# A fused RWKV, cosine-MoE and soft-MoE kernel: weight landing buffers, score matmuls in quarters, decayed state on another engine, and a new order list

## The chip, the cores and the metric

The kernel runs on one core of one Trainium2 chip. The metric is the device time of one execution in microseconds. Three runs of the kernel before took 516.99, 517.70 and 518.56 us; the median is 517.7 us. The engines are named as in the profile: PE (matrix multiply) with its weight loads PEld, DVE (vector), ACT (scalar, with the function tables), POOL, and SP, whose queue issues every DMA of this kernel.

## The reference

Three stages follow each other. All inputs are float32 but the two MoE weights `w_in` and `w_out`, which come as float64.

```python
def _attn_ref(r, k, v, w, u):            # B=4, H=8, S=768, D=48
    for t in range(S):
        cur = einsum('bhd,bhe->bhde', u[None] * kt, vt)
        y[:, :, t] = einsum('bhd,bhde->bhe', rt, state + cur)
        state = wt[..., None] * state + einsum('bhd,bhe->bhde', kt, vt)

def _moe_ref(x, w_in, w_out):            # x: 3072 tokens x 384, d_ff = 2048
    h = x @ w_in
    return (h * cos(h)) @ w_out

def _moe2_ref(x, phi, w1, w2):           # 8 experts, 4 slots each
    logits = x @ phi
    d = softmax(logits, axis=0);  slot_input = d.T @ x
    slot_out[e] = relu(slot_input[e] @ w1[e]) @ w2[e]
    return softmax(logits, axis=1) @ slot_out
```

## The kernel before, in words

The first load is `cs`, the constants (identity, masks). **Attention** runs over 24 blocks of 128 tokens (`j` = 0 to 23, six to a batch), each as two chunks of 64. For a block the steps are: loads of w, k, r, v (`lw lk lr lv lz`), PE transposes of them (`wT kT rT`, four 128x128 transposes each, one PSUM bank each), products of decays by two DVE scans (`scan`, `sp`), scaled keys and receptances (`ks`, `L`), scores `A` (16 matmuls of 64x64 by 64 columns), the masking of the scores into the tile `lt` (`mask`, two `copy_predicated` of 64 partitions by 512, line 214), the transposed keys (`kN`, `ksn`), the chunks' outer products `U` (16 matmuls, two banks, line 239), the decayed state `z` (line 248, one DVE product of 128x192 for each chunk, but a memset for the first chunk of a batch), its copy into `rzs` by ACT (`rz`), the state's update by DVE (`st`, line 256, which reads a bank of `U` and `z`), and the block's output `y` (32 matmuls of 32 columns each), which ACT and DVE split into a high and a low part (`xh`, `xl`).

**The MoE** takes each block's tokens as soon as they are there: for each of 24 token tiles `t` and four banks `q` of 512 features, `h.t.q` (nine matmuls of 512 columns, lines 421 to 423), then ACT, DVE, ACT, DVE (`turns rest cos mul`) make h cos(h), PE transposes it (`gT`), ACT copies it (`gc`) and PE multiplies it by a projection to the 32 slots (`l`). Softmax steps over tokens (`sum lc max exp xt xr xd dT dc ltok E es`) follow for each 256 tokens. After the list, an end part works out the experts and the outputs.

**The weights** come as float64 bit pairs and are decoded on the chip: ACT takes the high word's magnitude (`abs`), DVE shifts it, puts the sign in and joins the low word's bits (`d1 d2a d2b`, lines 329, 334, 342); `w_in` is then split into a rounded part (`whi`, ACT) and a rest (`wn` on PE, `wc` on ACT) that fill the tiles `wu0` to `wu3`, one for each bank `q`. `w_in` lands in eight pieces of 256 columns (the first of them in two halves) in a ring of two raw buffers, one half in the place of `wu0`; of `w_out`, four pieces land two by two in the places of `wu2` and `wu3` and four in the ring. `w_out` pieces are decoded into `wo_sb`, transposed (`oT`, `oc`) and projected (`om pc pT ps`).

**Order.** The text `HEAD` is a list of 1896 steps, written out; it is run through from front to back under a manual schedule, so each engine's queue, and SP's with its DMAs, holds its instructions in the order of the list. A queue works strictly in its order; an instruction waits in front of its queue until its inputs are there and its buffer is free. PSUM's eight banks are parted into pools; most attention steps (`wT kT rT kN A U y`, and `wn oT pT`) share the pool `ps_a` of three banks:

```python
ps_h = ...tile_pool(name="ps_h", bufs=2, space=PSUM)    # h
ps_t, ps_l, ps_m: one bank each                          # gT, l, softmax
ps_a = ...tile_pool(name="ps_a", bufs=3, space=PSUM)     # attention, weights
```

Of the kernel before, what the change touches and what calls it, by code (L numbers as in the profile page):

```python
# [21 lines left out]
def rwkv_moe_kernel(ctx: ExitStack, tc: tile.TileContext, r, k, v, w, u, w_in, w_out, phi, w1, w2, cst, out):  # L22
    nc = tc.nc
# [266 lines left out]
    raw_t, a_t, pt_ps, wt_t = {}, {}, {}, {}  # L290

    def part(t, hf):

        if hf is None:
            return t
        t = t.rearrange("p (k f) t -> p k f t", k=KD) if len(t.shape) == 3 else t.rearrange("p (k f) -> p k f", k=KD)
        return t[:, :, hf * 128:(hf + 1) * 128]

    def e_raw(x, n, hf=None):

        if x == "i":
            if hf:
                raw_t[x, n, hf] = wu_p.tile([128, 4 * DM, 2], I32, tag="wu0", name=f"rawi{n}b")[:, 0:768, :]
            else:
                raw_t[x, n, hf] = raw_p.tile([128, 768, 2], I32, tag="raw", name=f"rawi{n}")
            src = w_in[:, n * 256:(n + 1) * 256].bitcast(I32).rearrange("(k p) f -> p k f", p=128)
            dst = raw_t[x, n, hf].rearrange("p (k f) t -> p k (f t)", k=KD)
            if hf is not None:
                src, dst = (v[:, :, hf * 256:(hf + 1) * 256] for v in (src, dst))
            nc.sync.dma_start(dst, src)  # L310
        elif n < 4:
            t = wu_p.tile([128, 4 * DM, 2], I32, tag=f"wu{3 - n // 2}", name=f"rawo{n}")
            src = w_out[n * 256:(n + 2) * 256, :].bitcast(I32).rearrange("(q p) n -> p q n", p=128)
            nc.sync.dma_start(t.rearrange("p (q n) t -> p q (n t)", q=4), src)
            raw_t[x, n, None], raw_t[x, n + 1, None] = t[:, 0:768, :], t[:, 768:1536, :]
        else:
# [555 lines left out]
wc.0.0 st.1.0 wn.0.1 d2b.o.1 z.1.1 abs.o.0 abs.o.2 rz.1.0 y.0 d1.o.0 st.1.1 wc.0.1 d2a.o.0 sr.2 oT.2 ru.2 oc.2 oT.3 xh.0 oc.3 d2b.o.0 rz.1.1 kT.2
d1.o.2 xl.0 oT.1 ks.2 lv.3 oT.0 sp.2 y.1 abs.i.1 oc.1 d2a.o.2 d1.i.1 oc.0 kN.2 d2b.o.2 wT.3 om.0 wf.3 xh.1 d2a.i.1 xl.1 oT.4 ksn.2 oT.5 oc.4 U.2
d2b.i.1 oc.5 z.2.0 raw.i.3 st.2.0 lw.5 whi.1 abs.i.4 z.2.1 bo.2 rT.2 bs.2 st.2.1 L.2 wn.1.0 wc.1.0 lz.3 d1.i.4 wn.1.1 wc.1.1 d2a.i.4 rz.2.0 oT.7
scan.3 A.2 abs.i.3 d2b.i.4 d1.i.3 lk.3 D.2 mask.2 d2a.i.3 raw.i.6 h.0.0 oc.7 whi.4 wn.4.1 d2b.i.3 rz.2.1 wc.4.1 kT.3 turns.0.0 wn.4.0 lw.4 whi.3 lr.3
pc.0 ru.3 abs.i.6 sr.3 raw.i.5 ks.3 wc.4.0 oT.6 sp.3 oc.6 d1.i.6 wn.3.0 rest.0.0 wc.3.0 wn.3.1 lk.4 d2a.i.6 rT.3 wT.4 d2b.i.6 wc.3.1 L.3 z.3.0 wf.4
whi.6 cos.0.0 h.1.0 abs.i.5 scan.4 pT.0 raw.i.7 turns.1.0 wn.6.1 d1.i.5 wc.6.1 wn.6.0 bo.3 wT.5 mul.0.0 wc.6.0 sr.4 d2a.i.5 h.0.1 abs.i.7 d2b.i.5 sp.4
whi.5 bs.3 lz.2 A.3 ps.0 turns.0.1 lr.4 rz.3.0 y.2 wf.5 D.3 xh.2 om.1 rest.1.0 d1.i.7 kN.3 cos.1.0 mask.3 ksn.3 wn.5.0 rest.0.1 cos.0.1 wc.5.0 wn.5.1
mul.1.0 raw.o.4 gT.0.0 wc.5.1 d2a.i.7 kT.4 xl.2 lz.4 d2b.i.7 mul.0.1 abs.o.4 whi.7 U.3 pc.1 ks.4 ru.4 raw.o.5 st.3.0 h.0.2 wn.7.0 d1.o.4 turns.0.2
z.3.1 gc.0.0 d2a.o.4 wn.7.1 rest.0.2 wc.7.1 st.3.1 h.1.1 rT.4 gT.0.1 cos.0.2 abs.o.5 wc.7.0 scan.5 turns.1.1 d2b.o.4 bo.4 lw.6 oT.8 oc.8 mul.0.2  # L880
rest.1.1 sr.5 kN.4 d1.o.5 h.0.3 bs.4 cos.1.1 L.4 mul.1.1 pT.1 rz.3.1 d2a.o.5 lk.5 ksn.4 gc.0.1 y.3 turns.0.3 h.1.2 rest.0.3 oT.9 xh.3 ps.1 cos.0.3
raw.o.7 lv.4 d2b.o.5 oT.11 gT.0.2 z.4.0 turns.1.2 oc.11 lr.5 oc.9 D.4 xl.3 oT.10 oc.10 A.4 rest.1.2 U.4 mul.0.3 l.0.0 sp.5 l.0.1 st.4.0 mask.4 abs.o.7
lw.7 lr.6 z.4.1 om.2 cos.1.2 pc.2 gc.0.2 raw.o.6 mul.1.2 abs.o.6 h.2.0 ru.5 gT.0.3 rz.4.1 rT.5 gc.0.3 pT.2 d1.o.6 h.1.3 ps.2 rz.4.0 d1.o.7 st.4.1 wT.6
d2a.o.6 d2b.o.6 turns.1.3 wf.6 L.5 kT.5 gT.1.1 lz.5 ks.5 d2a.o.7 gc.1.1 lr.7 lw.8 lv.5 oT.12 oT.13 turns.2.0 kN.5 oc.12 d2b.o.7 close rest.1.3 lk.6
bo.5 ksn.5 z.5.0 gT.1.0 l.0.2 gc.1.0 oc.13 A.5 oT.14 gT.1.2 oT.15 bs.5 scan.6 oc.14 D.5 l.1.0 l.1.1 oc.15 cos.1.3 gc.1.2 mul.1.3 ru.6 y.4 rest.2.0
om.3 h.2.1 pc.3 xh.4 pT.3 cos.2.0 mask.5 gT.1.3 bo.6 xl.4 turns.2.1 wT.7 ps.3 U.5 l.1.2 sr.6 mul.2.0 gc.1.3 lv.6 l.0.3 sp.6 rz.5.0 st.5.0 wf.7 l.1.3
z.5.1 sum.0 rz.5.1 rest.2.1 h.2.2 scan.7 rT.6 gT.2.0 cos.2.1 mul.2.1 turns.2.2 L.6 rest.2.2 gc.2.0 kT.6 h.2.3 lk.7 lc.0 bs.6 ks.6 cos.2.2 turns.2.3
sr.7 gT.2.1 lz.6 mul.2.2 kN.6 z.6.0 ksn.6 st.5.1 D.6 rest.2.3 ru.7 gc.2.1 max.0 sp.7 exp.0 A.6 xt.0 U.6 gT.2.2 lr.8 h.3.0 xr.0 xd.0 cos.2.3 st.6.0
bo.7 dT.0 ltok.0 dc.0 mul.2.3 lk.8 gc.2.2 y.5 z.6.1 turns.3.0 l.2.0 rest.3.0 mask.6 l.2.1 xh.5 cos.3.0 E.0.0 h.3.2 rT.7 st.6.1 rz.6.0 xl.5 turns.3.2
rz.6.1 mul.3.0 wT.8 kT.7 L.7 ks.7 gT.2.3 h.3.1 ru.8 rest.3.2 gc.2.3 gT.3.0 A.7 lv.8 E.0.1 l.2.2 bs.7 turns.3.1 z.7.0 bo.8 wf.8 cos.3.2 rest.3.1 y.6  # L890
D.7 lw.10 scan.8 lv.7 lr.9 l.2.3 gc.3.0 mul.3.2 lw.9 l.3.0 cos.3.1 sr.8 kN.7 es.0 sp.8 xh.6 ksn.7 mask.7 mul.3.1 bs.8 h.3.3 rT.8 L.8 kT.8 gT.3.2 h.4.1
# [112 lines left out]
```

## Time and profile before

| | |
|---|---|
| median of three runs | 517.7 us |
| profiled execution | 517.14 us, span 515.4 us, granted clock 0.991 |
| PE busy | 481.4 us, 93% of the span |
| DVE busy | 426.2 us, 83% |
| ACT busy | 318.7 us, 62% |
| POOL busy | 100.2 us, 19% |
| DMA | 67.47 MB, 131 GB/s on average |

Busy time is the time in which at least one instruction of the engine is under way, so a matmul that streams behind another is not counted twice. PE's busy share is low in the first slices of the span and in the last ones; between, it is at 90% or more in every slice. An execution's own time is a little more than its span (517.14 against 515.4 us).

### The profile page before, as it was taken

The page shows a single profiled execution, that of the slowest core. Times are in us where ns is not written, and L with a number is a line of the kernel's source. Part 1 is how long each engine was busy: PE and PEld are TensorE (multiplying, and loading weights), DVE is VectorE, ACT ScalarE, POOL GpSimd, SP SyncE. Part 2 cuts the span into 40 slices and gives each one's busy share as a digit, 9 for nine tenths or more (in the row PEclk, how much of TensorE's full clock was granted, in tenths as well). Part 3 has the DMA queues.
Part 4 walks back from the last instruction along what each step waited for, and adds up shares of the span by engine and source line. Part 5 has one row for each costly group of instructions (what it writes and reads, how often), then busy time and mean ns, then how long its engine had stood idle before and what let it go on. Part 6 is the DMA issues. An engine that isn't in the chain of part 4 may idle for free.

```text
span 515.4 us, 15516 instructions
## 1 busy us (share of the span) xinstructions
PE 481.4 (93%) x6515; PEld 378.3 (73%) x6515; DVE 426.2 (83%) x809; ACT 318.7 (62%) x703; POOL 100.2 (19%) x127
## 2 busy tenths in 40 slices
...
GB/s 208 313 191 139 198 166 203 139 66 45 100 67 68 59 36 93 18 51 76 48 108 4 62 73 23 108 48 95 25 56 17 350 369 39 102 294 336 400 174 269
DMA packets 146325, 67.47 MB, mean 131 GB/s; under 512 B 127184, under 2 KB 134352, under 8 KB 146256
## 3 DMA queue, kind: packets, MB, share of 16 engines
...
q8 instruction: 51, 0.84, 0.7%
q14 instruction: 18, 0.15, 0.1%
...
## 4 chain that ended last, share of the span: by engine, by line
PE 53%; DVE 7%; ACT 3%; issue 1%
PE h L421 9%; PE h L423 8%; PE h L422 8%; PE gT L455 6%; PE l L470 3%; PE E L566 3%; PE A L193 2%; PE hps L754 2%; PE so L794 2%; PE y L267 2%; PE U L239 1%; DVE g L440 1%; PE o L827 1%; PE rT L134 1%; PE kT L134 1%; DVE lt L214 1%
## 5 line engine op out<-in xcount | busy, mean ns | idle before, releaser
L421 PE MATMUL h<-wu,x 128*128 128x512 f32 x288 | 121.4, 422 | 1.4 <-DVE g L448 1.3
L423 PE MATMUL h<-wu,x 128*128 128x512 f32 x288 | 113.2, 393 | 0.0
L422 PE MATMUL h<-wu,x 128*128 128x512 f32 x288 | 112.6, 391 | 0.0
L444 ACT ACTIVATE g<-g,half_pi 128x512 f32<-128x512 f32 (+1 forms) x97 | 69.2, 719 | 32.2 <-DVE g L440 31.6
L436 ACT ACTIVATE g<-h 128x512 int32<-128x512 f32 (+1 forms) x96 | 56.6, 595 | 51.8 <-PE h L423 41.9
L440 DVE SCALAR_TENSOR_TENSOR g<-g,h 128x512 f32<-128x512 int32 (+1 forms) x96 | 64.5, 675 | 18.0 <-ACT g L436 17.6
L448 DVE TENSOR_TENSOR g<-g,h 128x512 f32<-128x512 f32 (+1 forms) x96 | 64.7, 675 | 13.3 <-ACT g L444 12.3
L207 POOL TENSOR_SCALAR_AFFINE_SELECT lt<-bo 64x512 f32<-64x512 f32 x48 | 37.3, 778 | 159.4 <-ACT bo L230 89.6
L421 PEld LDWEIGHTS h<-wu,x 128*128 128x128 f32 x288 | 54.2, 188 | 16.5 <-issue 3.5
L461 ACT COPY gt<-gT 128x512 f32<-128x512 f32 x89 | 51.8, 585 | 19.1 <-PE gT L455 15.7
L423 PEld LDWEIGHTS h<-wu,x 128*128 128x128 f32 x288 | 54.0, 188 | 12.3
L422 PEld LDWEIGHTS h<-wu,x 128*128 128x128 f32 x288 | 54.4, 189 | 8.7
L455 PE MATMUL gT<-cs,g 128*128 128x128 f32 x384 | 57.5, 275 | 0.2
L162 POOL TENSOR_TENSOR ru<-rn,u_b 128x384 f32<-128x384 f32 x24 | 26.2, 1092 | 133.8 <-DMA rn<-in_r_dram 82.9
L455 PEld LDWEIGHTS gT<-cs,g 128*128 128x128 f32 x384 | 44.7, 141 | 8.2 <-issue 1.9
L214 DVE COPY_PREDICATED lt<-cs,A 64x512 f32<-64x512 uint32 x48 | 35.4, 737 | 1.6 <-POOL lt L207 0.3
L253 ACT COPY rzs<-z 64x192 f32<-64x192 f32 x96 | 33.4, 348 | 4.1 <-DVE z L248 3.0
L149 DVE TENSOR_TENSOR_SCAN qt<-wf,one_b 128x520 f32<-128x520 f32 x24 | 30.4, 1267 | 5.8 <-ACT wf L144 5.7
L178 DVE TENSOR_TENSOR lt<-rT,pt 64x512 f32<-64x512 f32 x48 | 32.8, 683 | 0.8 <-PE rT L134 0.2
L470 PE MATMUL l<-gt,p_sb 128*32 128x128 f32 x768 | 30.7, 276 | 0.3 <-DVE gt L461 0.3
L193 PE MATMUL A<-lt,ks 64*64 64x64 f32 x768 | 28.0, 224 | 3.0 <-DVE st_state L256 1.6
L157 DVE TENSOR_TENSOR_SCAN pt<-wf,ini_f 128x520 f32<-128x520 f32 x24 | 30.1, 1256 | 0.1
...
## 6 DMA issues: line engine op xcount, KB each, us to landing
...
rawi<-in_moe_w_in_dram SPq DMA_DIRECT2D x7, 768.0 KB, 5.0
wn<-in_w_dram SPq DMA_DIRECT2D x24, 192.0 KB, 4.4
kn<-in_k_dram SPq DMA_DIRECT2D x24, 192.0 KB, 4.0
rn<-in_r_dram SPq DMA_DIRECT2D x24, 192.0 KB, 3.9
vn<-in_v_dram SPq DMA_DIRECT2D x24, 192.0 KB, 3.8
...
```

Of the source, the lines that this page charges most:

```text
L193: nc.tensor.matmul(ps[64 - 64 * a:128 - 64 * a, s, :], lhsT=ks[k, s, :], rhs=L[k, a, s, :], start=True, stop=True)
L214: nc.vector.copy_predicated(out=lt[j % 2][h, a], mask=mask[h].bitcast(U32).unsqueeze(1).to_broadcast([64, NS, C]), data=ps[h])
L421: nc.tensor.matmul(half[:, f], lhsT=xh[:, c, :], rhs=wh, start=(c == 0), stop=False)
L422: nc.tensor.matmul(half[:, f], lhsT=xl[:, c, :], rhs=wh, start=False, stop=False)
L423: nc.tensor.matmul(half[:, f], lhsT=xh[:, c, :], rhs=wl, start=False, stop=(c == KD - 1))
L436: nc.scalar.activation(gt.bitcast(I32), hp, AF.Copy, bias=0.25, scale=1.0 / TWO_PI)
L440: nc.vector.scalar_tensor_tensor(out=gt, in0=gt.bitcast(I32), scalar=-TWO_PI, in1=hp, op0=ALU.mult, op1=ALU.add)
L444: nc.scalar.activation(gt, gt, AF.Sin, bias=half_pi[:, 0:1])
L448: nc.vector.tensor_tensor(out=gt, in0=gt, in1=hp, op=ALU.mult)
L455: nc.tensor.transpose(ps[:, m * 128:(m + 1) * 128], gt[:, m * 128:(m + 1) * 128], ident)
L461: (nc.vector.tensor_copy if n >= ATT and n % 8 in (1, 2, 5) else nc.scalar.copy)(gt_t[t, q], pend.pop(("gT", t, q)))
L470: nc.tensor.matmul(lps_t[g][32 * m:32 * m + 32, o:o + TB], lhsT=p_sb[:, 4 * q + m, :], rhs=gt[:, m * 128:(m + 1) * 128], start=first, stop ...
```

## The change

Four things change.

1. `w_in` lands by bank in a tile of its own, which takes the place (the tag) of the later `wu` tile of that bank: bank 0 in two DMAs of 256 columns, banks 1 to 3 in one DMA of 512 columns each. `w_out` lands in eight pieces, all through the ring of two. The decode works on whole pieces, with a ring of four decoded tiles (`dec` has 4 buffers, was 2).
2. From block 6 on (`JA = 6`) the scores `A` go to two banks and, for every second segment, to the other 64 output partitions, so that all four pairs of a row half and a column half of the array occur in turn. `mask` is then four `copy_predicated` of 64x256 in place of two of 64x512.
3. From block 8 on (`JZ = 8`) `z` is four ACT instructions of 128x48 with a scale for each partition, in place of one DVE product of 128x192.
4. `HEAD` is a new order of 1890 steps.

```diff
+    JZ = 8
+    JA = 6
-    dec = d_stack.enter_context(tc.tile_pool(name="dec", bufs=2))
+    dec = d_stack.enter_context(tc.tile_pool(name="dec", bufs=4))
     def e_A(j):
-        ps = tps(f"A{j}").rearrange("p (s j) -> p s j", j=C)
+        ps = [tps(f"A{j}_{a}" if j >= JA else f"A{j}").rearrange("p (s j) -> p s j", j=C) for a in range(1 if j < JA else 2)]
         for s in range(NS):
             for a in range(2):
                 k = slice(64 * a, 64 * a + 64)
-                nc.tensor.matmul(ps[64 - 64 * a:128 - 64 * a, s, :], lhsT=ks[k, s, :], rhs=L[k, a, s, :], start=True, stop=True)
+                o = 64 * a if j >= JA and s % 2 else 64 - 64 * a
+                out = ps[0][o:o + 64, s] if j < JA else ps[a][o:o + 64, s // 2]
+                nc.tensor.matmul(out, lhsT=ks[k, s, :], rhs=L[k, a, s, :], start=True, stop=True)
     def e_mask(j):
         for a in range(2):
             h = slice(64 - 64 * a, 128 - 64 * a)
+            if j < JA:
+                ...
+            for c in range(2):
+                o = slice(64 * a, 64 * a + 64) if c else h
+                nc.vector.copy_predicated(out=lt[j % 2][h, a, c::2], mask=..., data=ps[a][o, 0:HP])
     def e_z(j, c):
-            nc.vector.tensor_tensor(out=z, in0=st_state, in1=pc[:, :, c, :].to_broadcast([128, HP, D]), op=ALU.mult)
+            if j < JZ:
+                nc.vector.tensor_tensor(out=z, in0=st_state, in1=pc[:, :, c, :].to_broadcast([128, HP, D]), op=ALU.mult)
+            else:
+                for p in range(HP):
+                    nc.scalar.activation(z[:, p], st_state[:, p], AF.Copy, scale=pc[:, p, c])
+    def e_raw(x, n):
+        if x == "i":
+            q, f = n // 2, slice((n % 2) * 256, (n % 2) * 256 + 256) if n < 2 else slice(0, 512)
+            if q not in rawi_t:
+                rawi_t[q] = wu_p.tile([128, KD * 512, 2], I32, tag=f"wu{q}", name=f"rawi{q}")...
+            ...
+            nc.sync.dma_start(t.rearrange("p k f t -> p k (f t)")[:, :, 2 * f.start:2 * f.stop], src)
+        else:
+            t = raw_p.tile([128, 768, 2], I32, tag="raw", name=f"rawo{n}")
+            ...
 HEAD = """
-lw.0 lk.0 raw.i.2 z.0.0 wT.0 lw.1 kT.0 wf.0 scan.0 raw.i.0.0 abs.i.2 ks.0 sr.0 sp.0 d1.i.2 d2a.i.2 wT.1 lr.0 misc kN.0 ru.0 wf.1 scan.1 ksn.0 d2b.i.2
+raw.i.0 abs.i.0 d1.i.0 raw.i.1 lk.0 lw.0 abs.i.1 raw.i.2 d2a.i.0 d2b.i.0 d1.i.1 d2a.i.1 wT.0 lr.0 wf.0 d2b.i.1 kT.0 lw.1 whi.1 z.0.0 scan.0 lv.0
 ...
-bs.11 rest.7.3 st.11.0 cos.7.3 h.8.0 mul.7.3 kT.12 sp.12 turns.8.0 bs.12 rest.8.0 lw.13 ks.12 h.7.2 z.11.1 gc.7.1 cos.8.0 mul.8.0 lv.13 gT.7.0 D.11
+U.11 gT.6.3 rest.7.3 cos.7.3 h.7.0 st.11.0 mul.7.3 cmb.0.1 h.8.0 kT.12 z.11.1 turns.7.0 cmb.0.4 sp.12 gc.6.3 lv.12 rest.7.0 gT.7.1 cos.7.0 xl.9
 ...
```

## Rows read from the trace of the kernel before

**Rows 1.** Windows: length, busy us (x instructions) by engine, granted clock, DMA share, GB/s.

```profile
0.00:13.00 13.00, 5.04 (x20) 3.72 (x20) 6.40 (x9) 4.91 (x8) 3.65 (x22) 1.00 0.98 207
13.00:77.00 64.00, 50.00 (x651) 35.24 (x652) 61.57 (x92) 40.11 (x82) 19.52 (x18) 0.97 0.84 202
77.00:182.00 105.00, 104.92 (x1476) 86.34 (x1476) 96.66 (x175) 72.21 (x160) 24.29 (x26) 1.00 0.48 92
182.00:286.00 104.00, 103.12 (x1440) 82.97 (x1439) 93.44 (x183) 67.66 (x153) 22.62 (x27) 1.00 0.33 56
...
468.00:515.40 47.40, 38.82 (x626) 26.83 (x626) 17.20 (x42) 14.57 (x36) 6.68 (x10) 0.94 0.81 285
```

**Rows 2.** Timeline of the front: start, duration, engine, line, operation, idle before.

```profile
4.77 1.09 PE L134 MATMUL wT<-cs,wn 128*128 128x128 f32 x4 [4.77 <-DMA wn<-in_w_dram]
...
6.65 1.24 DVE L149 TENSOR_TENSOR_SCAN qt<-wf,one_b 128x520 f32<-128x520 f32 x1 [5.52 <-ACT wf L144]
...
76.72 0.50 PE L421 MATMUL h<-wu,x 128*128 128x512 f32 x1
```

**Rows 3.** Chain that ended last, in order of time: start, duration, what.

```profile
201.05 0.61 PE U L239 x32
201.66 0.94 PE A L193 x32
202.60 0.59 PE gT L455 x4
...
208.00 0.44 PE gT L455 x4
208.79 0.89 PE y L267 x64
...
292.27 1.08 PE A L193 x32
```

**Rows 4.** Groups by line and form: count, busy us, mean ns, idle before.

```profile
L448 DVE TENSOR_TENSOR g<-g,h 128x512 f32<-128x512 f32 x95 | 64.3, 678 | 13.1 <-ACT g L444 12.3
...
L214 DVE COPY_PREDICATED lt<-cs,A 64x512 f32<-64x512 uint32 x48 | 35.4, 737 | 1.6 <-POOL lt L207 0.3
L253 ACT COPY rzs<-z 64x192 f32<-64x192 f32 x96 | 33.4, 348 | 4.1 <-DVE z L248 3.0
...
L248 DVE TENSOR_TENSOR z<-st_state,qt 128x192 f32<-128x192 f32 x44 | 19.4, 441 | 0.6
...
L230 ACT COPY bo<-bo 64x4 f32<-64x4 f32 x48 | 9.3, 193 | 1.4 <-DVE bo L225 0.3
...
L448 DVE TENSOR_TENSOR g<-g,h 128x256 f32<-128x256 f32 x1 | 0.4, 421 | 0.1
...
```

**Rows 5.** DVE's groups in the window 13 to 77 us: the decode of `w_in`.

```profile
L342 DVE SCALAR_TENSOR_TENSOR ai<-rawi,ai 128x768 int32<-128x768 int32 (+1 forms) x8 | 7.9, 983 | 0.1
L334 DVE SCALAR_TENSOR_TENSOR ai<-rawi,ai 128x768 int32<-128x768 int32 (+1 forms) x7 | 6.2, 886 | 0.0
...
L329 DVE TENSOR_SCALAR ai<-ai 128x768 int32<-128x768 int32 (+1 forms) x8 | 4.5, 568 | 0.4 <-ACT ai L325 0.3
```

**Rows 6.** DMA issues: size of one, median us from issue to landing.

```profile
rawi<-in_moe_w_in_dram SPq DMA_DIRECT2D x7, 768.0 KB, 5.0
wn<-in_w_dram SPq DMA_DIRECT2D x24, 192.0 KB, 4.4
...
cs<-in_const_dram SPq DMA_DIRECT2D x1, 160.0 KB, 2.4
```

**Rows 7.** Timeline around the scores of block 20.

```profile
353.15 0.68 PE L239 MATMUL U<-vn,ksn 64*64 64x48 f32 x32
...
353.65 1.11 PE L193 MATMUL A<-lt,ks 64*64 64x64 f32 x32
...
353.88 0.36 DVE L256 TENSOR_TENSOR st_state<-U,z 128x192 f32<-128x192 f32 x1
...
355.39 1.51 DVE L214 COPY_PREDICATED lt<-cs,A 64x512 f32<-64x512 uint32 x2
```

More of the change, by code (lines that the diff above doesn't have):

```diff
@@ L288, in rwkv_moe_kernel @@
     wu = {}
[L290 to L299, printed above, removed]
-        if x == "i":
[L302 to L315, printed above, removed]
+    raw_t, rawi_t, a_t, pt_ps, wt_t = {}, {}, {}, {}, {}
+    def e_raw(x, n):
+        if x == "i":
+            q, f = n // 2, slice((n % 2) * 256, (n % 2) * 256 + 256) if n < 2 else slice(0, 512)
+            if q not in rawi_t:
+                rawi_t[q] = wu_p.tile([128, KD * 512, 2], I32, tag=f"wu{q}", name=f"rawi{q}").rearrange("p (k f) t -> p k f t", k=KD)
+            t = rawi_t[q]
+            src = w_in[:, q * 512 + f.start:q * 512 + f.stop].bitcast(I32).rearrange("(k p) f -> p k f", p=128)
+            nc.sync.dma_start(t.rearrange("p k f t -> p k (f t)")[:, :, 2 * f.start:2 * f.stop], src)
+            for i in (n,) if n < 2 else (n, n + 1):
+                raw_t[x, i] = t[:, :, (i % 2) * 256:(i % 2) * 256 + 256, :]
         else:
@@ L872 @@
[L872 to L891, printed above, removed]
@@ L956 @@
[L956 removed]
+raw.i.0 abs.i.0 d1.i.0 raw.i.1 lk.0 lw.0 abs.i.1 raw.i.2 d2a.i.0 d2b.i.0 d1.i.1 d2a.i.1 wT.0 lr.0 wf.0 d2b.i.1 kT.0 lw.1 whi.1 z.0.0 scan.0 lv.0
+abs.i.3 misc ks.0 rT.0 wT.1 kN.0 sr.0 raw.i.4 abs.i.2 sp.0 wf.1 d1.i.3 ru.0 d2a.i.3 L.0 d1.i.2 scan.1 ksn.0 wn.1.1 U.0 lr.1 d2b.i.3 whi.0 wc.1.1
+st.0.0 lk.1 lw.2 wn.0.0 wn.1.0 wc.0.0 d2a.i.2 wn.0.1 sr.1 z.0.1 wc.1.0 d2b.i.2 st.0.1 bo.0 rT.1 abs.i.5 sp.1 wc.0.1 A.0 bs.0 wT.2 lv.1 d1.i.5 whi.2
@@ new lines @@
+L.1 kT.1 raw.o.0 abs.i.4 D.0 mask.0 lk.2 wf.2 whi.3 ks.1 ru.1 wn.2.1 kN.1 rz.0.0 rz.0.1 wn.2.0 ksn.1 wc.2.1 lz.0 wc.2.0 d1.i.4 raw.i.6 d2a.i.5 z.1.0
+d2a.i.4 scan.2 lr.3 U.1 abs.o.0 st.1.0 y.0 bo.1 xh.0 wn.3.1 lr.2 z.1.1 lz.1 raw.o.1 lw.3 d1.o.0 st.1.1 d2b.i.5 d2a.o.0 d2b.i.4 wc.3.1 wn.3.0 rz.1.0
+bs.1 xl.0 whi.4 A.1 kT.2 rz.1.1 abs.i.7 h.0.0 d2b.o.0 D.1 wc.3.0 whi.5 lw.4 ru.2 mask.1 abs.i.6 wn.4.1 wc.4.1 d1.i.7 ks.2 oT.0 wn.4.0 y.1 oc.0 wc.4.0
+wn.5.1 d2a.i.7 sr.2 z.2.0 raw.o.2 sp.2 turns.0.0 lv.2 lk.3 h.0.1 d1.i.6 lk.4 xh.1 lz.2 rest.0.0 d2b.i.7 d2a.i.6 abs.o.1 cos.0.0 wc.5.1 xl.1 turns.0.1
@@ new lines @@
+wn.5.0 bo.2 abs.o.2 wc.5.0 d1.o.1 mul.0.0 d2b.i.6 kN.2 oT.1 d2a.o.1 oc.1 d1.o.2 ksn.2 wT.3 whi.7 rT.2 whi.6 d2b.o.1 rest.0.1 h.1.0 wf.3 rz.2.0 oT.2
+L.2 lr.4 oc.2 turns.1.0 U.2 scan.3 wn.7.0 st.2.0 sr.3 oT.3 cos.0.1 wc.7.0 oc.3 raw.o.3 z.2.1 abs.o.3 sp.3 d2a.o.2 mul.0.1 gT.0.0 wn.6.1 wc.6.1 st.2.1
+A.2 rest.1.0 wn.6.0 bs.2 rz.2.1 rT.3 d2b.o.2 D.2 L.3 mask.2 gc.0.0 h.0.2 kT.3 wc.6.0 wn.7.1 lv.3 ks.3 gT.0.1 wT.4 d1.o.3 kN.3 cos.1.0 z.3.0 ru.3
+turns.0.2 om.0 wf.4 bo.3 ksn.3 wc.7.1 gc.0.1 y.2 d2a.o.3 rest.0.2 oT.5 oc.5 cos.0.2 mul.1.0 lz.3 bs.3 lw.5 oT.4 scan.4 A.3 D.3 xh.2 d2b.o.3 mask.3
@@ new lines @@
+h.3.3 rz.6.0 cos.3.1 turns.3.3 mask.7 rz.7.0 gT.3.2 ks.8 U.7 mul.3.1 lr.9 y.6 sr.8 rest.3.3 st.7.0 gc.3.2 D.8 l.2.3 lk.9 l.3.0 h.4.1 rT.8 cos.3.3
+mul.3.3 gT.3.1 z.7.1 xh.6 xl.6 es.0 h.4.0 sp.8 turns.4.1 st.7.1 lr.10 gc.3.1 rest.4.1 rz.7.1 L.8 gT.3.3 cos.4.1 turns.4.0 wT.9 A.8 l.3.1 gc.3.3
+rest.4.0 l.3.2 wf.9 cos.4.0 l.3.3 z.8.0 ru.10 kN.8 mul.4.1 sum.1 mask.8 gT.4.1 h.4.2 mul.4.0 ksn.8 bo.10 kT.9 lc.1 rz.8.0 ru.9 scan.9 U.8 turns.4.2
+lv.10 rest.4.2 st.8.0 ks.9 gc.4.1 max.1 cos.4.2 gT.4.0 h.5.0 exp.1 lk.11 sr.9 z.8.1 mul.4.2 xt.1 xr.1 turns.5.0 lz.8 h.4.3 st.8.1 wT.10 rT.9 gc.4.0
```

174 lines of the change are left out of this document (90 added, 84 removed).

## The prediction

> **What bounds the kernel now.** I read the busy shares by engine first, then the windows by stage, then the timeline of the front and the chain of waits. Outside the front and the end PE is the bound: it idles 0.08 us of 105 between 77 and 182 us and 0.88 of 104 after that, with DVE beside it at 90 to 92% and ACT at 65 to 69% [rows 1]. So there a microsecond of PE work is worth a microsecond, if DVE keeps up. In the front it is otherwise: PE idles 22.0 of the first 77 us, while DVE, after 6.6 idle us in the first 13, is busy for 61.57 of the next 64 [rows 1]. PE's waits there end on DVE's work, and PE is full from about h.0.2, at 76.72 us [rows 2]. The list has 102 DVE instructions ahead of h.0.2 and the windows count 101 up to 77 us, so h.0.2 comes when DVE is through with what stands ahead of it. The time is therefore a front, in which DVE decides how much PE time is lost; a middle that is PE's own work; and an end of 47 us behind the list [rows 1], which the change does not touch.
>
> **The change part by part.** The sum is made against the profiled execution, 517.14 us (span 515.4). The median shown is 517.7, so 0.6 is added at the end.
>
> *Scores in quarters, blocks 6 to 23 (18 blocks).* A block's A has 32 matmul records, issued two at a time, and takes 0.94 us behind U [rows 3]. U, as many records on 64x64 pieces of the array, but on four of them in turn, takes 0.61, of which 0.14 is the change of form: A behind U takes 0.94 and A behind a transpose 1.08 [rows 3]. So U's eight groups of four take 0.47. U streams 48 columns and A 64; y streams 64 columns and takes 0.89 for 16 groups of four, 0.056 a group [rows 3], so eight groups are 0.45 with 64 columns too. I take 0.47 for the new A: 0.47 less for each block, 18 x 0.47 = 8.5 us. The lower end, if time grew with columns from U's, is 0.63 and 5.6 us in all; no gain at all is a rival.
>
> The Trainium skill speaks against this: "TensorE: Matmul & The Clock Gate", Part 3, "The mechanism", says that a weight load overlaps matmuls in flight only when the row group differs. The new order puts both column halves of a row half within each group of four, so by this rule these would go one behind the other, A would keep its 0.94, and this term would be 0 in place of 8.5. U has the same pattern and its 0.61 [rows 3] does not show such a wait, so the trace disagrees.
>
> *What the quarters cost.* In the list before, A and U of a block stand side by side on PE in 15 of the 18 blocks and share the form; in the new list never. Each pair that is parted pays once more to enter, 0.14, and to leave: gT takes 0.59 behind A and 0.44 else, 0.15 [rows 3]. That would be 15 x 0.29 = 4.4 us, but the whole list has fewer changes of form (282 in place of 290), as h and the narrow matmuls alternate less. Between 0 and 4.4 I take 2.0. Mask: a 128x256 DVE product takes 421 ns and a 128x512 one 678, so half of the columns saves 257; a quarter mask is 737 - 257 = 480, and four less two of 737 make 0.45 us more on DVE for a block, 8 us in 18 blocks [rows 4]. It lies beside PE's work; DVE has 8 to 10% free there [rows 1].
>
> *z on ACT, blocks 8 to 23.* 32 less two memsets are 30 products off DVE, 30 x 0.441 = 13.2 us [rows 4], more than the mask adds. On ACT come 120 small instructions, each between 193 ns (64x4) and 348 (64x192) [rows 4]; with 48 columns they are near the low end, 0.2, so 24 us, into an engine with over 30% free [rows 1]. Neither decides, so both are 0 in the sum. What the four ACT instructions do add is a wait: z stands in ACT's queue behind cosines and copies of gT, st on DVE waits for z, and st holds U's banks. If no other PE work covers that wait, it is rival D below.
>
> *The front: landing and order.* Ahead of h.0.2 the new list has 84 DVE instructions in place of 102; at 61.57 / 92 = 0.67 us each [rows 1] that is 12.0 us earlier. But less PE work is then done too: five sets of four transposes fewer (0.44), four w_out transposes (three quarters of 0.44), two projections (priced as y, 0.89, the nearest row), a y, a U and an A, and one weight product of about 1.1 more: 6.5 us [rows 3]. So 5.5 us less PE time is lost by then. PE must also stay full behind it: ahead of h.3.0 it is 165 in place of 172 DVE instructions, 7 x 0.6 (between 0.67 and the next window's 96.66 / 175 = 0.55) = 4.2 us earlier, with 1.8 us less PE work (two gT, an A): 2.4 us. The smaller decides if DVE stays the bound. DVE may start later: first come cs and half a bank of w_in, and with the other half they stand ahead of the first loads of k and w on SP's queue. At 207 GB/s [rows 1], cs, two halves and two loads, 160 + 2 x 768 + 2 x 192 KB [rows 6], take 10.3 us, so wT.0 starts near 11 us, not at 4.77, and the first scan near 13, not at 6.65 [rows 2]. Until then DVE decodes two halves, 2 x (0.57 + 0.89 + 0.98) = 4.9 us [rows 5]; its idle time in the first 13 us stays at about 7. I take 2.5 us for the front, between 1.5 and 5.5. The rings: w_in waits for no raw buffer any more, whi overwrites the landing tile and so waits for both decodes of its bank, which stand ahead of it on DVE in the list; w_out pieces 2 to 7 wait on SP's queue for the ring, with the loads of blocks 2 to 6 behind them, and each such piece stands in the list behind the decode that frees its buffer. Both at 0.
>
> *Banks.* A takes two of the three banks of ps_a and U two, so A and U of a block no longer fit together. In the new list 2.6 to 13.3 us of other PE work lies between them, but 0.5 to 0.8 in blocks 10, 12 and 20. For these and for z's wait I add 1.0 us of PE idle, twice what a 105 us window had on average [rows 1].
>
> Sum: -8.5 + 2.0 - 2.5 + 1.0 = -8.0; 517.1 - 8.0 = 509.1, and 0.6 for the median: about 509.5.
>
> **The rivals.**
>
> *A, everything comes.* The front gives 5.5 and the parting of A and U costs nothing: 517.7 - 8.5 - 5.5 = 503.7. For it: fewer changes of form, the DVE count at h.0.2. Against: h.3.0's count. Chance 0.15.
>
> *B, the late tokens decide the front.* The attention chain starts 6.2 us later and DVE starves for it: the front costs up to 6.2 in place of giving 2.5, so between 512.0 (front at nothing) and 518.2. For it: PE's first waits are for loads [rows 2], and the DMA engines are at 0.98 in the first 13 us [rows 1]. Against: DVE has decode to do meanwhile. Chance 0.15.
>
> *C, the quarters don't overlap.* Then A keeps 0.94: 509.5 + 8.5 = 518.0, the page's rule as a mechanism of this kernel. Against it stands U. Chance 0.05.
>
> *D, slower: the banks.* Block 20 shows the hold: U issued at 353.15, its first bank free when st ends at 354.24; A issued at 353.65, its bank free when the masks end at 356.90 [rows 7]. If each A or U must wait for the other's release, a block pays at least U's 1.1 us: 18 x 1.1 = 20 us, so 517.7 - 9.0 + 20 = 529; with z late behind ACT's queue, more. The gain, 6.5 + 2.5, is 0.5 us a block, so it decides from a mean wait of 0.5. For it: the pool does not grow. Against: the PE work that the list puts between the two. Chance 0.10.
>
> **How the numbers follow.** The forecast has 0.55; its own range is 506 to 513 (the front between 1.5 and 5.5, the forms between 0 and 4.4, the quarters at 5.6 or more). The 8-in-10 range takes in A and most of B and C: 502.5 to 517.5. A measurement here can tell about 0.3%, 1.6 us, from no change. Faster: the forecast, A and two thirds of B, 0.80, with 0.01 of D; same: 0.05 of B and 0.03 of C and 0.01 of D, 0.09; slower: the rest of C and D, 0.10.
>
> **What the profile after would show.** A on the chain at about 0.6 behind another form, and its group of 768 records near 18 to 20 us busy, not 28; h.0.2 at 64 to 68 us; wT.0 near 11 us; PE idle under 1 us in each window of 100 us from there; masks of about 0.48; ACT over 70% busy. The prediction is wrong if A stays at 0.94, if PE waits for A's or U's banks (the release by mask or st) for over half a microsecond a block, or if h.0.2 comes later than 72 us.

## Result and profile after

The changed kernel is 0.75% slower: 521.03 us (median of 9 runs, 518.99 to 522.73) against 517.42 us of the kernel before in the same measurement; the ratio is 1.0075 [1.006, 1.009]. The forecast was 509.5. The profiled execution took 521.62 us, span 519.9, granted clock 0.992.

The windows of the changed kernel, to be laid beside [rows 1] (columns as there):

```profile
0.00:13.00 13.00, 0.00 (x0) 0.00 (x0) 1.89 (x3) 3.58 (x5) 3.31 (x21) 1.00 0.67 174
13.00:77.00 64.00, 52.17 (x622) 38.23 (x623) 62.68 (x91) 42.02 (x83) 17.55 (x15) 0.97 0.87 206
77.00:182.00 105.00, 101.25 (x1503) 81.60 (x1502) 96.02 (x175) 74.64 (x180) 32.13 (x32) 1.00 0.50 96
182.00:286.00 104.00, 101.51 (x1424) 81.37 (x1423) 92.18 (x181) 77.95 (x199) 19.45 (x22) 1.00 0.32 57
286.00:390.00 104.00, 102.80 (x1554) 81.96 (x1553) 94.01 (x189) 78.80 (x202) 24.34 (x25) 1.00 0.31 55
390.00:468.00 78.00, 75.82 (x766) 58.91 (x757) 56.19 (x124) 49.61 (x111) 2.23 (x4) 1.00 0.52 189
468.00:519.90 51.90, 41.63 (x661) 28.33 (x661) 20.02 (x53) 17.85 (x46) 6.68 (x10) 0.96 0.84 300
```

PE does nothing in the first 13 us and DVE 1.89 us, not 6.40. Between 77 and 182 us PE idles 3.75 us where it idled 0.08, and 2.49 in place of 0.88 after that. PE's busy time over the whole span fell from 481.4 to 475.2 us; its idle time (span less busy) rose from 34.0 to 44.7.

The front on the timeline (start, duration, engine, line, operation, idle before), to be laid beside [rows 2]:

```profile
1.25 5.88 SPq L313 DMA_DIRECT2D rawi<-in_moe_w_in_dram  x2
...
5.85 0.89 ACT L324 ACTIVATE ai<-rawi 128x768 f32<-128x768 f32 x1 [2.38 <-DMA rawi<-in_moe_w_in_dram]
6.77 0.56 DVE L328 TENSOR_SCALAR ai<-ai 128x768 int32<-128x768 int32 x1 [6.77 <-ACT ai L324]
7.18 0.49 SPq L119 DMA_DIRECT2D kn<-in_k_dram  x1
7.71 0.58 SPq L119 DMA_DIRECT2D wn<-in_w_dram  x1
...
11.64 0.96 DVE L333 SCALAR_TENSOR_TENSOR ai<-rawi,ai 128x768 int32<-128x768 int32 x1 [4.31 <-DMA rawi<-in_moe_w_in_dram]
...
13.80 0.45 PE L136 MATMUL wT<-cs,wn 128*128 128x128 f32 x1 [13.80 <-DMA wn<-in_w_dram]
```

SP issues two halves of `w_in` in 5.88 us, where one issue takes about half a microsecond: the second waits, and leaves only after ACT's read of the first half (5.85 to 6.74) is over. The loads of k and w stand behind it and leave at 7.18 and 7.71. DVE waits 4.31 us for a transfer, though its step reads only the half that ACT has read already. h.0.2 starts at 67.16 us, not at 76.72.

The chain of the changed kernel, to be laid beside [rows 3], and its groups by form beside [rows 4]:

```profile
223.37 0.62 PE A L197 x32
...
248.35 0.44 PE gT L452 x4
248.79 0.62 PE A L197 x32
```

```profile
L223 DVE COPY_PREDICATED lt<-cs,A 64x256 f32<-64x256 uint32 x72 | 32.2, 447 | 2.4 <-PE A L197 0.9
L261 ACT ACTIVATE z<-st_state,qt 128x48 f32<-128x48 f32 x120 | 30.1, 324 | 2.1 <-DVE st_state L269 2.0
L197 PE MATMUL A<-lt,ks 64*64 64x64 f32 x768 | 19.3, 223 | 0.2 <-ACT wt L378 0.2
...
L258 DVE TENSOR_TENSOR z<-st_state,qt 128x192 f32<-128x192 f32 x14 | 4.8, 342 | 0.0
```

A in quarters takes 0.62 us on the chain, as forecast, and waits for a bank almost never (0.2 us in all). What PE waits for between 77 and 468 us (us, times, longest) is small and spread out:

```profile
PE h L418 <- DVE g L445: 3.0, 5, 1.4
PE kT L136 <- DMA kn<-in_k_dram: 1.4, 1, 1.4
PE l L467 <- issue: 1.4, 1, 1.4
```

### The profile page after: what moved, and what is told of

Read it like the earlier page. It is cut to its first block, busy times and chain, and to the rows that moved or that the text cites. A ratio compares the mean times of both kernels' runs of the same rounds, so it can differ in the third digit from the quotient of the medians.

```text
span 519.9 us, 15660 instructions
## 1 busy us (share of the span) xinstructions
PE 475.2 (91%) x6515; PEld 370.4 (71%) x6515; DVE 423.0 (81%) x812; ACT 344.5 (66%) x822; POOL 105.7 (20%) x127
## 4 chain that ended last, share of the span: by engine, by line
PE 64%; DVE 22%; ACT 5%; DMA 4%; issue 3%; SPq 0%; DVEq 0%; ACTq 0%
PE h L418 10%; PE h L420 9%; PE h L419 9%; PE gT L452 6%; PE l L467 4%; PE E L563 3%; PE y L280 3%; DMA rawi<-in_moe_w_in_dram 3%; DVE g L445 2%; DVE g L437 2%; PE A L197 2%; PE hps L751 2%; PE so L791 2%; PE U L248 2%; DVE pt L159 2%
## 5 line engine op out<-in xcount | busy, mean ns | idle before, releaser
L445 DVE TENSOR_TENSOR g<-g,h 128x512 f32<-128x512 f32 x96 | 64.7, 677 | 12.8 <-ACT g L441 11.9
L211 POOL TENSOR_SCALAR_AFFINE_SELECT lt<-bo 64x512 f32<-64x512 f32 x48 | 38.8, 808 | 176.6 <-ACT bo L239 81.6
L418 PEld LDWEIGHTS h<-wu,x 128*128 128x128 f32 x288 | 54.2, 188 | 17.7 <-DVE g L445 7.4
L164 POOL TENSOR_TENSOR ru<-rn,u_b 128x384 f32<-128x384 f32 x24 | 29.4, 1225 | 109.4 <-DVE bo L234 40.6
L223 DVE COPY_PREDICATED lt<-cs,A 64x256 f32<-64x256 uint32 x72 | 32.2, 447 | 2.4 <-PE A L197 0.9
L261 ACT ACTIVATE z<-st_state,qt 128x48 f32<-128x48 f32 x120 | 30.1, 324 | 2.1 <-DVE st_state L269 2.0
```

The costliest lines, as they stand in the source:

```text
L211: nc.gpsimd.affine_select(out=lt[j % 2][h, a], in_=bo_t[j][h, a].unsqueeze(2).to_broadcast([64, NS, C]), pattern=[[0, NS], [-1, C]], compa ...
L418: nc.tensor.matmul(half[:, f], lhsT=xh[:, c, :], rhs=wh, start=(c == 0), stop=False)
L445: nc.vector.tensor_tensor(out=gt, in0=gt, in1=hp, op=ALU.mult)
```

## The experiments

Times are medians of 6 to 12 runs beside the kernel before on the same chip, ratios are against that kernel. Its own medians beside these runs lay between 517.08 and 517.67 us, so a difference between two kernels measured apart is good to about 0.6 us. Within the runs of one kernel of the new order, a mean granted clock lower by 0.001 mostly went with 0.3 to 0.6 us more; where two kernels' runs differ in it, that is said. Edits are of the changed kernel unless said otherwise.

### e1_halves: the false wait in the front

```diff
+            if n < 2:
+                t = t.rearrange("p k f t -> p (k f t)").rearrange("p (h k f t) -> p h k f t", h=2, k=KD, t=2)[:, n]
```

> The changed kernel with one view altered: the two halves of the first w_in bank lie one behind the other in their landing buffer, not interleaved row group by row group. In the changed kernel the second half's DMA is held on SP until ACT has read the first half (it waits for the abs), and DVE's second decode step waits for both halves; here neither wait is in the program. Theory F (this wait is the loss of the front): first PE instruction at 10 to 11.5 us in place of 13.80, DVE idle in the first 13 us near 7 in place of 11.1, and 3 to 4 us come back: 517 to 518.3, against 521.0 of the changed kernel. Rival (the middle gives the time away whatever the front hands it, because another engine paces it): first PE instruction as early, but under 1 us comes back: 520 to 521.

Measured: 517.88 us, 1.0003 [0.9989, 1.0017]. Theory F holds: 3.1 us came back. Its front:

```profile
1.26 0.95 SPq L316 DMA_DIRECT2D rawi<-in_moe_w_in_dram  x2
2.25 0.49 SPq L119 DMA_DIRECT2D kn<-in_k_dram  x1
2.78 1.53 SPq L119 DMA_DIRECT2D wn<-in_w_dram  x1
...
7.34 0.56 DVE L331 TENSOR_SCALAR ai<-ai 128x768 int32<-128x768 int32 x1 [7.34 <-ACT ai L327]
7.93 0.96 DVE L336 SCALAR_TENSOR_TENSOR ai<-rawi,ai 128x768 int32<-128x768 int32 x1
...
10.84 1.09 PE L136 MATMUL wT<-cs,wn 128*128 128x128 f32 x4 [10.84 <-DMA wn<-in_w_dram]
```

Both halves are issued in 0.95 us, DVE goes from step to step, wT.0 starts at 10.84, and DVE idles 7.6 of the first 13 us, as I had forecast for the change. In the changed kernel the halves lie interleaved in one tile (each of the three groups of 128 rows of `w_in` holds first one half, then the other), and what was read and what is written were taken to overlap, though no byte is shared. Laid one behind the other, the wait is gone.

### e2_z_dve, e3_pairs, e4_order: the parts of the change taken back

```diff
-    JZ = 8
+    JZ = 99
-    JA = 6
+    JA = 99
```

(e2 has the first edit, e3 the second, e4 both.)

> The changed kernel with the decayed state on DVE in all blocks (the other two parts kept). ACT loses 120 instructions of 321 ns less what it did before, about 26 us (344 to 318 us busy), DVE gains 30 x 0.44 = 13 us. Theory Z (z in ACT's queue is what makes the middle late: turns, cosines and copies of gT stand behind it, st waits for it): 517 to 519, PE idle between 77 and 390 us under 3 us in place of 7.4. Rival D (DVE paces the new order, and z on ACT relieves it): 522 to 526. Rival A (neither engine decides, the two banks of A do): 520 to 522.

> The changed kernel with A in pairs in one bank in all blocks, as before, in the new order and with z on ACT. PE has about 18 x 0.4 = 7.5 us more work, DVE 18 x (4 x 0.448 - 2 x 0.737) = 5.7 us less. If the quarters give what their PE time says: 526 to 529. Theory B (the second bank of A is what costs the time, as ps_a has three): the waits go and pay for the work, 519 to 521.5. If DVE paces the middle, the two nearly cancel: 521 to 524.

> The changed kernel with A in pairs and the decayed state on DVE in all blocks: the landing and the new order alone; each instruction is then as in the kernel before, whose time is 517.4. Theory O (the order itself has less slack, and loses the front's late start besides): 523 to 528, that is slower than the changed kernel, as it has neither the 7.5 us of PE work saved nor the 13 us of DVE work moved. Theory Z or B (z on ACT or A's second bank cost the time): 516 to 520.

Measured: e2 525.87 us, 1.0167 [1.0143, 1.0191]; e3 522.49 us, 1.0098 [1.0076, 1.0120]; e4 526.96 us, 1.0170 [1.0145, 1.0196]. Theory Z falls and rival D's band is met: z on ACT is worth 4.8 us in the new order. Theory B falls too: the quarters gain, though 1.5 us only, which is in the band for a middle that DVE paces. (The intervals of e3 and of the changed kernel overlap, and e3's runs had a mean clock of 0.9940 against 0.9914; at an equal clock I estimate 2.5 us.) Theory O holds: the order and the landing alone, with A and z as before, cost 9.3 us (526.96 against 517.67). That list was made for quarters and for z on ACT, so not all of this is a price of the order as such.

### e5_loads: what stands behind the w_out pieces on SP's queue

Edit (on e1_halves): raw.o.6 stands behind lr.5, raw.o.7 behind lr.6.

> e1_halves with two loads moved on SP's queue: the w_out pieces 6 and 7, which wait there until a landing buffer of the ring of two is decoded, now stand behind the loads of v, k and r for blocks 4 to 6 that stood behind them. In e1_halves PE waits 1.17 us for k of block 5 at 94.7 us, and the load was issued at 87.9, right behind the last of these pieces. Theory R (the ring's hold on SP's queue is a part of what the middle lost): the wait for k goes, 1 to 2 us come back, 516 to 517, against 517.9 for e1_halves. Rival (DVE paces that stretch anyway): the wait goes and the time stays, 517.4 to 518.4.

In e1_halves the timeline shows the hold (three pieces take SP 16.29 us, as each waits for its buffer) and what it does to PE:

```profile
64.69 16.29 SPq L322 DMA_DIRECT2D rawo<-in_moe_w_out_dram  x3
...
87.45 0.40 SPq L322 DMA_DIRECT2D rawo<-in_moe_w_out_dram  x1
87.90 0.45 SPq L119 DMA_DIRECT2D kn<-in_k_dram  x1
```

```profile
94.66 0.63 PE L136 MATMUL kT<-cs,kn 128*128 128x128 f32 x4 [1.17 <-DMA kn<-in_k_dram]
```

Measured: 515.10 us, 0.9957 [0.9939, 0.9976]: 2.8 us back, a little more than the theory said. Some 0.7 us of it may be the clock (a mean of 0.9928 against e1_halves' 0.9908, an estimate with e13_moves' 0.36 us for 0.001). In its trace k of block 5 is issued at 78.91, nine microseconds sooner, and PE's wait is gone:

```profile
62.05 9.43 SPq L322 DMA_DIRECT2D rawo<-in_moe_w_out_dram  x2
...
78.50 0.37 SPq L322 DMA_DIRECT2D rawo<-in_moe_w_out_dram  x1
78.91 0.47 SPq L119 DMA_DIRECT2D kn<-in_k_dram  x1
```

### e6_before_z: z on ACT in the old order

Edit (on the kernel before): the four ACT products of the change from j = 8 on.

> The kernel before, in its own order, with one part of the change alone: the decayed state on ACT from the ninth block on. DVE loses 13 us of work (30 products of 0.44), ACT gains about 26 us. If DVE paces the middle in the old order as in the new one, where this part was worth 4.9 us: 512.5 to 514.5. If the middle is PE's own work, as I predicted: 517 to 518, no change. If ACT's queue is what is late: 519 or more.

Measured: 521.85 us, 1.0091 [1.0071, 1.0110]. The same edit that gains 4.8 us in the new order costs 4.6 in the old. DVE's own work fell from 426.2 to 416.9 us, but between 160 and 430 us DVE waits 4.7 us for z, which it did not before, and 22.9 us for ACT's turns and cosines, in place of 17.7. First the kernel before, then e6 (us, times, longest):

```profile
DVE g L440 <- ACT g L436: 11.4, 16, 1.8
DVE g L448 <- ACT g L444: 6.3, 10, 1.0
```

```profile
DVE g L444 <- ACT g L440: 13.9, 19, 1.8
DVE g L452 <- ACT g L448: 9.0, 13, 1.9
DVE st_state L260 <- ACT z L252: 4.7, 6, 1.5
```

In the changed kernel the same waits are 2.2 us for z and 10.6 us for turns and cosines. So the third expectation holds, ACT's queue is what is late, and "DVE paces" was too simple: what z costs depends on where the list puts it on the queue that runs it.

### e7_before_half and e10_half_2masks: half of A's work in the old order

Edit of e7 (on the kernel before; e10 keeps the two masks, which then read the first chunk's scores twice):

```diff
+            if j >= 6 and s % 2:
+                continue
             for a in range(2):
...
+            for c in range(2):
+                nc.vector.copy_predicated(out=lt[j % 2][h, a, c::2], ..., data=ps[h, 0::2])
```

`s` runs over the pairs of heads and, fastest, over the two chunks of a block. So the second chunk's scores are left out, and the first chunk's stand in for them; the "even heads" of the expectations are the first chunks.

> The kernel before, in its own order, with the price of the quarters and without their second bank: from the seventh block on A computes only the even heads (16 of 32 matmuls, so half of the scores is left out and the even ones stand in for the odd), and the masks are four of 64x256 in place of two of 64x512. PE loses 18 x 0.47 = 8.5 us, DVE gains 18 x 0.32 = 5.8 us. If the middle is PE's own work: 509 to 511. If DVE paces it: 516 to 518.

> e7_before_half (the kernel before in its own order; from the seventh block on A computes the even heads alone and they stand in for the odd ones) with the masks in two instructions of 64x512 again, so that PE's work falls as with quarters and DVE's does not grow: e7 ran 516.0 against 517.3 for the kernel before. Theory M (the four masks on DVE ate what PE saved): 509 to 511.5. Rival L (the engines go in lockstep in an order fixed for the old durations, and PE's saving turns into waits for turns, cosines and products): 514.5 to 516.5.

Measured: e7 515.98 us, 0.9972 [0.9958, 0.9985]; e10 515.55 us, 0.9975 [0.9961, 0.9988]. Both moved by 1.3 to 1.5 us. Without the added masks (e10) nothing more is gained, so theory M falls and the time is L's. The windows of e10:

```profile
77.00:182.00 105.00, 104.57 (x1415) 84.55 (x1413) 97.31 (x175) 72.11 (x161) 23.11 (x26) 1.00 0.48 92
182.00:286.00 104.00, 101.98 (x1348) 81.12 (x1348) 93.45 (x184) 68.20 (x154) 23.27 (x27) 1.00 0.35 57
286.00:390.00 104.00, 102.67 (x1450) 82.90 (x1449) 94.57 (x188) 69.92 (x158) 21.59 (x23) 1.00 0.34 59
```

PE, which idled 0.88 us in the second window before, idles 2.02, and 3.8 in place of 1.5 in the three together. From the start of one PE instruction to the next, A's share falls from 25.5 to 17.8 us, all of PE's work by 4.0 only: transposes, E, y and others beside it take 3.7 more. So 7.7 us less 3.7 less 2.3 leaves 1.7, near the 1.5 measured. L's waits are the smaller half of the loss; why the steps beside a shorter A take longer was not tried.

### e9_z_early: z on ACT from the second block on

Edit (on e1_halves): `JZ = 1`.

> e1_halves with the decayed state on ACT from the second block on, not from the ninth: 13 more products leave DVE (5 to 6 us between 25 and 165 us, where its busy share is highest), ACT takes 52 more instructions of 0.32 us, 17 us. If DVE paces the front and the middle: 514.5 to 516.5, against 517.9. If ACT's own queue (decode, copies of transposes) is as full there: 518 to 520.

Measured: 519.82 us, 1.0045 [1.0027, 1.0063], 1.9 us slower than e1_halves. Between 20 and 165 us DVE waits 4.7 us for z, where it waits for none in e1_halves. DVE's load is not what decides; as in e6, a step put on another engine without a place of its own in the order costs time.

### e11_front: the first loads first

Edit (on e5_loads): the list begins with lw.0 lk.0 raw.i.0 lr.0 raw.i.1 and has scan.0 and ks.0 ahead of the decode.

> e5_loads with the first steps in another order: the loads of w and k of block 0 ahead of the first half of w_in, that of r ahead of the second, and on DVE the first scan and ks ahead of the decode. In e5_loads PE waits 10.8 us for the first w and 3.2 for the first r. Theory F2 (the late tokens still cost in the front): first PE instruction at 4.8 to 6 us, DVE idle in the first 13 us under 7, 1 to 3 us come back: 512 to 514, against 515.1. Rival (DVE's count of work decides the front and the decode starts later instead): 514.8 to 516.5.

Measured: 515.07 us, 0.9961 [0.9946, 0.9976], as e5_loads. The mechanism came, the time did not: wT.0 starts at 4.66 us. First the front of e5_loads, then of e11_front:

```profile
0.00:13.00 13.00, 1.94 (x8) 1.57 (x8) 5.41 (x8) 4.64 (x7) 3.30 (x21) 1.00 0.91 264
13.00:77.00 64.00, 53.85 (x673) 40.38 (x674) 62.51 (x97) 44.59 (x90) 21.61 (x18) 1.00 0.91 208
```

```profile
0.00:13.00 13.00, 3.74 (x14) 2.60 (x15) 5.99 (x9) 4.17 (x6) 3.29 (x21) 1.00 0.91 245
13.00:77.00 64.00, 53.86 (x654) 38.84 (x655) 61.88 (x91) 43.48 (x87) 18.47 (x18) 0.97 0.85 204
```

PE is busy 1.8 us longer by 77 us, and yet has run fewer instructions (668 for 681), at a granted clock of 0.97 in place of 1.00. But the profiled execution of e11 took 516.69 us, its longest, and that of e5 513.89, its shortest; over all runs the mean clocks are alike (0.9932 and 0.9928), so the clock does not explain the equal medians. Theory F2 falls, the rival's band is met, and its mechanism, DVE's count of work, was not shown.

### e12_loads_pairs, e16_loads_z_dve: the parts taken back in the mended kernel

Edits (on e5_loads): `JA = 99` in e12, `JZ = 99` in e16.

> e5_loads with A in pairs in one bank in all blocks: what the quarters are worth where the front and the loads are mended. If the held loads hid a part of their worth: 518 to 521, against 515.1. If they are worth what e3_pairs showed in the changed kernel (1.5 us): 516 to 517.3. If they are worth nothing here: 514.5 to 515.6.

> e5_loads with the decayed state on DVE in all blocks. In the changed kernel that cost 4.9 us. If DVE's load or the fit of the order to z on ACT is what it cost, it costs as much here: 519 to 521, against 515.1. If it was the late front of that kernel that made DVE scarce: 515.5 to 517.5.

Measured: e12 519.31 us, 1.0046 [1.0030, 1.0062]; e16 520.41 us, 1.0057 [1.0036, 1.0077]. The first theory of each holds: with the loads in time the quarters are worth 4.2 us, not 1.5, and z on ACT 5.3. At equal clocks the 4.2 and the 1.5 come closer (estimates of 3.8 and 2.5).

### e13_moves, e14_front_moves, e15_moves_pairs: three waits of the middle taken away

Edit (e13 on e5_loads, e14 on e11_front; e15 is e13 with `JA = 99`):

```diff
-... rest.8.2 cmb.0.2 D.12 ... mul.8.2 xl.10
+... rest.8.2 D.12 ... mul.8.2 cmb.0.2 xl.10
-... lc.5 max.5 h.12.3 exp.5 gc.12.0 mul.12.1
+... lc.5 mul.12.1 max.5 h.12.3 exp.5 gc.12.0
-... wT.6 sp.5 d2b.o.7 close xh.4 oc.13 xl.4
+... wT.6 d2b.o.7 close xh.4 oc.13 xl.4 sp.5
```

> e5_loads with three DVE steps moved in the list, at the three longest waits of PE between 77 and 300 us in its trace: a token-combination step (cmb.0.2) behind the product mul.8.2 in place of ahead of it (PE waits 1.40 us at 211 us for the bank that this product frees), the product mul.12.1 ahead of the maximum of group 5 (0.76 us at 287), and the second scan of block 5 (sp.5) behind the end of the decode and xl.4 (0.73 us at 98). Theory P (the middle loses at a few places where a queue has too little lead, and what is mended there stays): the three waits go and 1.5 to 2.9 us come back, 512.2 to 513.6, against 515.1. Rival L (in lockstep the time reappears at the next step): the waits go, and 514.5 to 515.5.

> e11_front with the three moves of e13_moves. Theory P (waits taken away in the middle give their time back): 512.5 to 514, against 515.1 for e11_front. Rival L (the time reappears at the next step): 514.5 to 516.5.

> e13_moves with A in pairs in one bank. In e5_loads the quarters were worth 4.2 us (e12_loads_pairs 519.3). If their worth grows as the middle's waits go: 521 to 523, against 516.4 for e13_moves. If it is the same: 519.5 to 521. If e13_moves had gained nothing in the middle for want of PE time: under 518.5.

Measured: e13 516.38 us, 0.9977 [0.9959, 0.9995]; e14 513.70 us, 0.9925 [0.9909, 0.9942]; e15 519.48 us, 1.0043 [1.0026, 1.0059]. The windows of e11_front, and then of e14_front_moves, from 182 to 390 us:

```profile
182.00:286.00 104.00, 101.52 (x1472) 81.61 (x1465) 92.20 (x182) 78.29 (x200) 21.20 (x24) 1.00 0.32 55
286.00:390.00 104.00, 102.92 (x1438) 82.04 (x1437) 93.22 (x190) 79.19 (x205) 24.76 (x27) 1.00 0.32 57
```

```profile
182.00:286.00 104.00, 103.02 (x1470) 82.75 (x1469) 92.74 (x182) 79.42 (x205) 23.90 (x27) 1.00 0.31 55
286.00:390.00 104.00, 103.55 (x1437) 82.51 (x1436) 92.23 (x190) 79.54 (x204) 22.12 (x24) 1.00 0.30 55
```

PE's idle time there fell from 3.56 to 1.43 us, and e14 is 1.4 us faster than e11, in theory P's band. e13 against e5 went the other way, by 1.3 us, and met neither band, though PE's idle in these two windows fell from 3.50 to 1.54 as well. The mean granted clock of e13's runs was 0.9900, of e5's 0.9928, and within e13's runs a clock lower by 0.001 goes with 0.36 us, so the clock accounts for 1.0 us of it. The same slope takes 0.5 us from e14's gain (0.9947 against e11's 0.9932).

The traces part the two. Up to the first step moved, e5 and e13 are the same program, and yet h.1.3 starts at 88.61 us in e5, whose clock between 13 and 77 us was 1.00, and at 92.19 in e13, where it was 0.95:

```profile
88.61 0.48 PE L421 MATMUL h<-wu,x 128*128 128x512 f32 x1
```

```profile
92.19 0.48 PE L421 MATMUL h<-wu,x 128*128 128x512 f32 x1
```

Up to 26 us the two run alike; e13 falls behind between 28 and 40 us, where its clock was low:

```profile
28.00:34.00 6.00, 3.55 (x13) 2.67 (x14) 5.96 (x11) 3.75 (x9) 2.70 (x3) 0.69 1.14 290
34.00:40.00 6.00, 6.00 (x113) 3.75 (x113) 4.57 (x8) 3.55 (x9) 0.12 (x1) 0.74 0.88 204
```

Between them lie e16 (1.00, 88.83) and e15 (0.97, 90.17), with the same steps up to there. From h.3.0 to the end e13 takes 398.4 us and e5 399.2, e14 397.8 and e11 399.8. So theory P holds behind the front, with 0.8 and 2.0 us in one profiled execution each, and e13's execution lost its gain ahead of it. e15 gives the quarters 3.1 us here, just under its band for an equal worth, so their worth did not grow with the waits gone. e14 beats both kernels: it is 0.75% faster than the one before, where the changed one is 0.75% slower.

## Why the prediction was wrong

The sum was -8.0 us, and the two profiles differ by +4.5. PE's own work was forecast right: -8.5 + 2.0 = -6.5 us, measured -6.2. Counted from start to start, A fell from 25.5 to 18.0 us, and all else rose by 1.3. The changes of form show in gT, 42.8 to 46.0 (45.5 in e3_pairs, so they come with the list and not with the quarters), but h fell from 208.8 to 205.7: that the 2.0 is near is a balance of terms, in part luck. PE's idle time was not forecast right: -2.5 + 1.0 = -1.5, measured +10.7. Of that, 2.9 us lie ahead of 77 us (22.0 to 24.8), 6.1 between 77 and 468 (3.5 to 9.6), 1.7 behind, each worked out from the windows (length less PE busy) of both kernels; two of the kernel before are not in [rows 1]:

```profile
286.00:390.00 104.00, 103.49 (x1556) 85.08 (x1555) 93.51 (x186) 70.03 (x159) 22.16 (x24) 1.00 0.34 58
390.00:468.00 78.00, 75.97 (x753) 58.16 (x751) 57.41 (x127) 49.19 (x108) 1.31 (x2) 1.00 0.57 214
```

Part by part, the forecast had -8.5 for the quarters, 0 for z and +0.5 for landing and list (-2.5 + 2.0 + 1.0). The runs show -1.5, -4.8 and +9.3 (3.0 together, against 3.6 measured for the change): the loss lies in the list and the landing, and the quarters gave too little against it. Three steps failed:

1. *The front, "its idle time in the first 13 us stays at about 7", wT.0 "near 11 us".* DVE idled 11.1 us and wT.0 started at 13.80. I had added up transfers as if all were issued at once, and missed that the second half waits for ACT's read of the first. e1_halves shows the size, 3.1 us, and that without it both numbers come out as forecast. Rival B had the right place and the wrong mechanism: mere late tokens cost nothing that can be told (e11_front). The reading that PE's waits in the front end on DVE's work was too simple too: of its 22.0 idle us there, 7.6 ended on loads of w.
2. *"The rings ... Both at 0."* I had checked that each w_out piece stands behind the decode that frees its buffer, so that nothing locks up, and took that for free. The loads of blocks 4 to 6 stood behind the waiting pieces on SP's queue; e5_loads shows 2.8 us, of which the clock may be 0.7; the trace shows one PE wait of 1.17 us gone.
3. *"A microsecond of PE work is worth a microsecond, if DVE keeps up", with z "Neither decides".* The quarters saved their PE time and got 1.5 us of it in the changed kernel, 3.1 and 4.2 in the mended ones (2.5 to 3.8 at equal clocks, by my estimate); in the old order as much PE work left out brought 1.3 to 1.5 (e7, e10). PE idling 0.08 us of 105 [rows 1] says that PE is full, not that nothing else is nearly so: DVE ran at 92% and ACT at 69% beside it in one fixed order, and a shorter A handed a part of its time to the steps beside it on PE and to waits for other engines (e10). The 1.0 us of idle that I added for banks and z was 6.1, a part of which is step 2's, and next to none of it is A waiting for a bank (0.2 us). z, costed at 0, was worth 4.8 to 5.3 us with the list made for it and cost 4.6 in the list made without. Its own duration was too low as well: 0.2 us, an estimate, against 0.324 measured, 30.1 us in place of 24; and what left DVE was less than 13.2 us, 9.3 in e6, as the mean of 441 ns holds a few long products (the median is 351, the longest 1776).

What the forecast said of the rest: masks near 0.48, measured 0.447; ACT over 70%, measured 71 to 76% between 77 and 390 us. h.0.2 came at 67.16, inside 64 to 68, and proves a poor sign: less work stood ahead of it, and that work was not done sooner.

Rival C fell. The rule of the Trainium skill that spoke for it ("TensorE: Matmul & The Clock Gate", Part 3, "The mechanism": a weight load overlaps only matmuls of another row group) would have kept A at 0.94; the chain has 0.62, so this trace does not show such a wait between column halves. Rival D, the banks, fell too: A waits for a bank 0.2 us in all, and e3_pairs, which gives it one bank, is no faster. Rival A assumed both things that failed. (517.1 - 8.0 + 0.6 makes 509.7; the 509.5 is rounded, and nothing hangs on it.)

Open remains what of the new order's 9.3 us (e4_order) is left when the false wait and the held loads, 5.9 us, are taken off, beyond the waits that e14 removed; those 5.9 were measured with the quarters and z in place, and the rest was not taken apart further.
